# A planned instruction order, fixed buffers and cheaper PSUM copies in a grouped-query attention backward kernel

## The chip, the cores and the metric

One core of a Trainium2 chip. The metric is the device time of one execution in microseconds (us); medians are over several executions, and "span" is the time from the first to the last instruction of the one profiled execution, some 2 us shorter than the device time. All times compared are of fast runs unless a run is named as slow. Engines: PE is TensorE, PEld its weight loads, DVE is VectorE, ACT is ScalarE, POOL is GpSimd, SP is SyncE. "Granted clock" is the share of TensorE's full clock that the throttle allowed.

## The reference, cut to what matters

```python
# B=32, Hq=32, Hkv=4, Sq=4, Sk=2048, D=128, all bf16
k = repeat(k, 8, axis=1); v = repeat(v, 8, axis=1)
p = softmax(einsum("bhqd,bhkd->bhqk", q, k) * D**-0.5)
out = einsum("bhqk,bhkd->bhqd", p, v)
# returned: out and the gradients of q, k, v for a given grad_out
```

Per batch, 32 query heads by 4 positions make 128 rows, so one batch is one set of 128 partitions, and each of the four K/V heads serves 32 of them. K, V, dK and dV are 2 MB each per batch: 8.52 MB go through the transfers per batch with the small tensors, 272.6 MB in all, half of it read and half written.

## The kernel before

Each batch runs through stages; a scheduler orders the instructions and chooses the copying engine (`nc.any`), and all PSUM tiles share one pool of eight banks.

```python
kv_pool = tile_pool(name="kv", bufs=12)      # ... kt 5, vt 8, e 2, et 2
o_pool  = tile_pool(name="ostage", bufs=4)   # dV and dK on their way out
ps_pool = tile_pool(name="ps", bufs=8, space=PSUM)

def pe_transpose_16(src_fn, dst):            # K, V, e and dS are transposed on PE
    for half in range(C // 8):
        tp = ps_pool.tile([P, 8, P], BF16, name="tp", tag="bk")
        for j in range(8):
            nc.tensor.transpose(out=tp[:, j, :], in_=src_fn(half * 8 + j), identity=ident[:])
        evac_big(dst[:, half * 8:half * 8 + 8, :], tp[:])   # nc.any.tensor_copy, 1024 bf16
# scores: four banks, reduce_max of each, reduce_max over four, POOL: negb = -scale * m, then exp
# O and dQ: four banks each, four small copies
# ... order of the stages:
stage_a1(0)
for b in range(B):
    stage_a2a(b)                             # scores, max, exp
    if b + 1 < B: stage_a1k(b + 1)           # next loads, K transposes (lower priority)
    stage_a2b(b); stage_b1o(b); stage_b1v(b) # e transposes, O, dV
    stage_b2a(b)                             # dP, dS
    if b + 1 < B: stage_a1v(b + 1)           # next V transposes (lower priority)
    stage_b2b(b)                             # dK, dQ
```

## Time and profile before

| | before |
|---|---|
| device time, median of the 4 first runs | 1014.98 us (1014.35 to 1016.63) |
| span of the profiled run, mean granted clock | 1012.6 us, 0.741 |
| busy: PE, DVE, ACT | 84%, 66%, 80% |
| moved | 269 GB/s over the span |
| time per batch (first to last score product, over 31) | 31.0 us |

The two rows below, of the page's 40 equal slices, are the shortest form of what the prediction reads from slices of one batch: digits are tenths, the first row of the granted clock, the second of the transfer engines' busy share.

```profile
PEclk9786887676777677776767776777767777677775
DMA  9898677687676686776786776866768767676244
```

Neither is ever steady: the trace's clock records read 0.50 and 1.00 by turns, 0.741 on average, and the transfers are idle over a quarter of the time (the page's queues take 35.8 + 35.6 + 0.7 + 0.1 = 72% of it).

### The profile page before, as it was taken

What the parts mean: (1) busy time and instruction counts of PE and PEld (TensorE: products, weight loads), DVE (VectorE), ACT (ScalarE), POOL (GpSimd) and SP (SyncE); (2) the same over time, 40 slices, a digit from 0 to 9 for tenths busy, and PEclk for the clock granted to TensorE, in tenths of its full rate; (3) what the DMA queues carried; (4) which work ended last, traced back from release to release, by engine and by line L of the source; (5) the groups of instructions that cost most, each with busy time, mean ns of one, the idle gap of its engine ahead of it and who ended that gap; (6) DMA issues with size and microseconds to landing.
All of it is one profiled execution on the core that took longest, in us unless ns stands there. A gap on an engine that the chain in (4) does not pass through costs nothing. (4 is left out here: it accounts for less than half of the span.)

```text
span 1012.6 us, 33638 instructions
## 1 busy us (share of the span) xinstructions
PE 848.5 (84%) x14400; PEld 618.8 (61%) x14400; DVE 668.8 (66%) x1283; ACT 805.1 (80%) x1406; POOL 185.8 (18%) x390
## 2 busy tenths in 40 slices
PE   6678788988889888889888889888898887988884
PEld 6456566666666665666565666656666565666553
DVE  5666667666667666677666676665766667666664
ACT  6688878788888878887878787777878778788874
POOL 0212112212122112122121222121221212212121
PEclk9786887676777677776767776777767777677775
DMA  9898677687676686776786776866768767676244
GB/s 353 314 352 299 255 293 275 262 313 282 252 304 250 268 334 257 259 300 248 299 313 252 281 272 266 309 251 260 284 256 307 263 249 276 262 304 229 112 170 169
DMA packets 85142, 274.82 MB, mean 271 GB/s; under 512 B 18432, under 2 KB 18432, under 8 KB 84992
## 3 DMA queue, kind: packets, MB, share of 16 engines
q1 hardware_dynamic: 46080, 136.34, 35.8%
q0 software_dynamic: 38912, 136.34, 35.6%
q8 instruction: 112, 1.84, 0.7%
q14 instruction: 38, 0.31, 0.1%
HBM read 136.31 MB, written 136.31 MB: 269 GB/s over the span
## 5 line engine op out<-in xcount | busy, mean ns | idle before, releaser
L101 ACT COPY kt_h<-tp 128x1024 bf16<-128x1024 bf16 x157 | 147.3, 1031 | 47.1 <-PE tp L82 46.3
L109 ACT CAST dv_h<-acc 128x512 bf16<-128x512 f32 x350 | 174.5, 641 | 0.8
L109 ACT CAST dk_h<-acc 128x512 bf16<-128x512 f32 x319 | 161.1, 643 | 17.0 <-DMA out_dram<-dv_h 15.9
L82 PEld LDWEIGHTS <-v_h 128*128 128x128 bf16 x2048 | 155.7, 119 | 25.8 <-issue 25.5
L82 PE MATMUL tp<-ident,v_h 128*128 128x128 bf16 x2048 | 161.3, 257 | 0.1
L101 ACT COPY vt_h<-tp 128x1024 bf16<-128x1024 bf16 x129 | 126.6, 1018 | 37.4 <-PE tp L82 37.3
L82 PEld LDWEIGHTS <-k_h 128*128 128x128 bf16 x2048 | 120.5, 100 | 35.7 <-issue 28.2
L82 PE MATMUL tp<-ident,k_h 128*128 128x128 bf16 x2048 | 130.0, 223 | 13.4 <-DMA k_h<-in_k_dram 6.9
L109 DVE CAST dk_h<-acc 128x512 bf16<-128x512 f32 x193 | 121.2, 683 | 27.8 <-DMA out_dram<-dv_h 21.1
L261 PE MATMUL acc<-dop_sb,e_sb 32*128 32x128 bf16 x2048 | 125.8, 281 | 14.5 <-ACT dv_h L109 2.6
L319 PE MATMUL acc<-qp_sb,ds_sb 32*128 32x128 bf16 x2048 | 94.1, 226 | 42.4 <-ACT dk_h L109 21.1
L82 PE MATMUL tp<-ident,e_sb 128*128 128x128 bf16 x512 | 67.4, 275 | 72.6 <-ACT e_sb L195 70.9
L329 POOL DMA_DIRECT2D out_dram<-dk_h x128 | 67.4, 533 | 310.6 <-ACT dk_h L109 296.1
L101 DVE COPY vt_h<-tp 128x1024 bf16<-128x1024 bf16 x127 | 84.7, 688 | 49.4 <-PE tp L82 47.7
L261 PEld LDWEIGHTS <-e_sb 32*128 32x128 bf16 x2048 | 65.3, 110 | 70.6 <-issue 65.6
L109 DVE CAST dv_h<-acc 128x512 bf16<-128x512 f32 x162 | 102.4, 682 | 1.0
L319 PEld LDWEIGHTS <-ds_sb 32*128 32x128 bf16 x2048 | 50.8, 95 | 82.6 <-issue 74.3
L82 PEld LDWEIGHTS <-e_sb 128*128 128x128 bf16 x512 | 38.3, 118 | 97.7 <-ACT e_sb L195 92.8
L291 DVE SCALAR_TENSOR_TENSOR ds_sb<-dp_q,delta,e_sb 128x512 bf16<-128x512 f32 x128 | 87.2, 743 | 9.8 <-PE dp_q L284 9.8
L195 ACT ACTIVATE e_sb<-s_q,negb 128x512 bf16<-128x512 f32 x128 | 86.3, 686 | 3.9 <-POOL negb L191 3.1
L271 POOL DMA_DIRECT2D out_dram<-dv_h x128 | 67.8, 536 | 104.2 <-ACT dv_h L109 98.3
L101 DVE COPY kt_h<-tp 128x1024 bf16<-128x1024 bf16 x99 | 67.5, 685 | 25.1 <-PE tp L82 24.1
(44 smaller groups left out, 938.9 us busy)
## 6 DMA issues: line engine op xcount, KB each, us to landing
k_h<-in_k_dram SPq DMA_DIRECT2D x128, 512.0 KB, 9.3
v_h<-in_v_dram SPq DMA_DIRECT2D x128, 512.0 KB, 5.7
out_dram<-dv_h POOLq DMA_DIRECT2D x128, 512.0 KB, 6.2
out_dram<-dk_h POOLq DMA_DIRECT2D x128, 512.0 KB, 6.5
q_sb<-in_q_dram SPq DMA_DIRECT2D x32, 32.0 KB, 2.6
do_sb<-in_grad_out_dram SPq DMA_DIRECT2D x32, 32.0 KB, 6.6
out_dram<-o_sb POOLq DMA_DIRECT2D x32, 32.0 KB, 5.5
out_dram<-dq_sb POOLq DMA_DIRECT2D x32, 32.0 KB, 9.5
```

The costliest lines, as they stand in the source:

```text
L82: nc.tensor.transpose(out=tp[:, j, :], in_=src_fn(c), identity=ident[:])
L101: nc.any.tensor_copy(out=out, in_=in_)
L109: nc.any.tensor_copy(out=out, in_=in_)
L195: nc.scalar.activation(out=e_sb[:, QW * cq:QW * cq + QW], in_=s_ps[cq][:], func=ACT.Exp, bias=negb[:], scale=scale, accum_out=l4[:, cq:cq ...
L261: nc.tensor.matmul(accs[h][:, j, :], lhsT=e_sb[32 * h:32 * h + 32, P * c:P * c + P], rhs=dop_sb[32 * h:32 * h + 32, :], start=True, stop=True,
L271: store_eng.dma_start(out=dv_v[b, h], in_=dv_sb[h][:].rearrange("p c d -> p (c d)"))
L291: nc.vector.scalar_tensor_tensor(out=ds_sb[:, QW * cq:QW * cq + QW], in0=dp_q[:], scalar=delta[:], in1=e_sb[:, QW * cq:QW * cq + QW], op0= ...
L319: nc.tensor.matmul(accs[h][:, j, :], lhsT=ds_sb[32 * h:32 * h + 32, P * c:P * c + P], rhs=qp_sb[32 * h:32 * h + 32, :], start=True, stop=True,
L329: store_eng.dma_start(out=dk_v[b, h], in_=dk_sb[h][:].rearrange("p c d -> p (c d)"))
```

## The change

Its intent: keep the mathematics, take the order of work away from the scheduler, and plan it. A list schedule is made in Python from a table of lengths, with due times per unit of work and a period of 21 us per batch; it gives the order of every queue, the PSUM bank of every tile and the engine of every copy. Beside it, three operations get cheaper. The core of the diff:

```diff
+PERIOD = 21.0
+LEN = dict(load=1.27, small=0.3, tr8=0.48, cp16=(0.61, 0.50), s=0.25, mx=0.66, m=0.1, ex=0.69,
+           l=0.75, o=0.45, oe=0.3, dl=0.4, ds=0.68, acc=0.40, cp32=(0.62, 0.50), qt=0.12, qte=0.3)
+CAP = dict(q=4, et=1, dt=1, k=12, v=9, kt=4, vt=4, out=13, e=3, ds=2)
+AT = dict(LQ=-44, LK=-42.0, LV=-25.0, QT=-17.0, KT=-19.5, VT=-3.5, S=0, DV=4.0, DK=13, DQ=14.5)
+    order, bank_of = plan(B)                      # ... list schedule, about 190 lines, cut
-    ps_pool = tile_pool(name="ps", bufs=8, space=PSUM)
+    ps_pool = pool("ps", 1, space=PSUM)           # tiles tagged by bank_of[...]
-            nc.any.tensor_copy(out=out, in_=in_)  # 1024 bf16
+        if on == "ACT":                           # 512 pairs read as fp32
+            nc.scalar.copy(out=out.rearrange(...).bitcast(FP32), in_=in_.rearrange(...).bitcast(FP32))
+        else:
+            nc.vector.tensor_copy(out=out, in_=in_)
-            nc.vector.reduce_max(out=m4[:, cq:cq + 1], in_=s_q[:], axis=AX.X)
-        nc.vector.reduce_max(out=m[:], in_=m4[:], axis=AX.X)
-        nc.gpsimd.tensor_scalar_mul(out=negb[:], in0=m[:], scalar1=-scale)
+            nc.vector.tensor_scalar(out=junk[:], in0=t["S", c][:], scalar1=-scale,
+                                    scalar2=t["m"][:] if c else None, op0=ALU.mult, op1=ALU.min,
+                                    accum_out=m[:])
-        o_ps = [ps_pool.tile([P, D], FP32, name="o_ps", tag="bk") for _ in range(NH)]
-        for h in range(NH):
-            evac_scalar(o_sb[32 * h:32 * h + 32, :], o_ps[h][...], rinv[...])
+            nc.vector.tensor_scalar(out=o[:], in0=t["O"][:, 0:D], scalar1=t["rinv"][:], ...)  # one bank
+    with tc.manual_schedule():
+        for u in order:
+            emit(u)
```

## The prediction

> **What bounds the kernel now.** I read first the page's busy shares, then the bytes that the DMA queues moved, then one batch cut into slices of 1 us, then the timeline of the same batch for what one instruction costs back to back, and last the costliest groups for the counts.
>
> ```profile
> PE 848.5 (84%) x14400; PEld 618.8 (61%) x14400; DVE 668.8 (66%) x1283; ACT 805.1 (80%) x1406; POOL 185.8 (18%) x390
> HBM read 136.31 MB, written 136.31 MB: 269 GB/s over the span
> L178 PE MATMUL s_q<-kt_h,qdt_sb x512: 379/631/634, 15.6 to 976.9; 128*32 128x512 bf16 x171
> ```
>
> No engine is full and the DMA average is far from what it reaches in bursts. The score matmuls (one group per batch) start at 15.6 us for the first batch and about 976 us for the last, so a batch takes 961/31 = 31.0 us. One batch in slices; the columns are the stretch, then the busy us (instructions) of PE, weight load, DVE, ACT and POOL, the granted clock, the DMA share and GB/s:
>
> ```profile
> 503.00:504.00 1.00, 0.93 (x22) 0.49 (x21) 1.00 (x2) 1.00 (x3) 0.00 (x0) 1.00 0.05 20
> 504.00:505.00 1.00, 0.69 (x20) 0.35 (x14) 0.68 (x2) 1.00 (x3) 0.00 (x0) 1.00 0.00 0
> 507.00:508.00 1.00, 1.00 (x44) 1.00 (x40) 0.00 (x0) 0.72 (x2) 0.97 (x2) 0.50 0.00 0
> 514.00:515.00 1.00, 0.00 (x0) 0.00 (x0) 0.30 (x2) 1.00 (x2) 0.00 (x0) 1.00 1.05 422
> 520.00:521.00 1.00, 1.00 (x39) 0.80 (x38) 0.00 (x0) 0.00 (x0) 0.00 (x0) 0.50 0.14 40
> 525.00:526.00 1.00, 1.00 (x13) 0.42 (x16) 0.67 (x2) 1.00 (x3) 0.00 (x0) 0.50 1.01 393
> 4.00:42.00 38.00, 27.43 (x486) 22.82 (x487) 24.18 (x44) 26.59 (x40) 3.27 (x7) 0.95 1.03 407
> ```
>
> The stages take turns. At 503 to 505 us DVE and ACT empty PSUM while DMA stands still; at 507 and 520 us PE works at half clock with both copy engines idle; at 514 us PE is idle behind the key-transpose copies on ACT. So the bound is the order of work and the buffers that separate the stages. The last row is the ceiling to remember: in the first 38 us DMA is never empty and moves 407 GB/s. (In the first few us there the clock column reads 1.00 before any record of it, while the transposes run at the cold rate.)
>
> What one instruction costs back to back (the mean duration hides an overlap, so I use run length; start, length, engine, line, what, count):
>
> ```profile
> 510.35 4.68 ACT L101 COPY kt_h<-tp 128x1024 bf16<-128x1024 bf16 x5 [1.25 <-PE tp L82]
> 502.70 5.01 ACT L109 CAST dk_h<-acc 128x512 bf16<-128x512 f32 x10
> 970.28 3.75 DVE L109 CAST dk_h<-acc 128x512 bf16<-128x512 f32 x6
> 20.74 2.57 DVE L101 COPY kt_h<-tp 128x1024 bf16<-128x1024 bf16 x4 [0.41 <-PE tp L82]
> 30.99 3.75 PE L82 MATMUL tp<-ident,v_h 128*128 128x128 bf16 x64
> 5.38 6.40 PE L82 MATMUL tp<-ident,k_h 128*128 128x128 bf16 x64 [5.38 <-DMA k_h<-in_k_dram]
> 24.94 1.08 PE L232 MATMUL o_ps<-v_h,et_sb 128*32 128x128 bf16 x64 [0.78 <-ACT et_sb L101]
> ```
>
> ACT: (4.68 - 1.03)/4 = 0.91 us per 1024-element copy, (5.01 - 0.64)/9 = 0.485 us per 512-element cast. DVE: (3.75 - 0.68)/5 = 0.614 us per cast, (2.57 - 0.69)/3 = 0.63 us per copy. PE: a transpose costs 59 ns warm and 100 ns cold.
>
> [...] the trace has 1031 and 641. Reading two bf16 as one fp32 must therefore almost halve ACT's copies. [...] the trace sustains 407 with peaks of 430, and I use 407. [...] the slices show 0.50 and 1.00, mean 0.741. [...] in the trace the first matmul of the next mode comes some 0.1 us late (my reading, at 16.6 and 35.5 us).
>
> **The change part by part.** It keeps the mathematics and PE's 14400 matmuls, and replaces the scheduler's order by a list schedule made in Python with a cost table, fixed queue order, an explicit PSUM bank per tile, an engine per copy, and other buffer counts (k 12, v 9, output 13 instead of 4).
>
> 1. ACT copies of transposes as fp32 pairs. The built order of the changed kernel puts 393 of 640 on ACT and 247 on DVE (before: 351 and 289), and of the 1024 accumulator casts 637 on ACT and 387 on DVE (before 669 and 355).
> 2. O and dQ go into one bank each and leave in one DVE instruction instead of four small ones on both engines (256 of about 0.36 us become 64).
> 3. The maximum comes with its sign and scale from one DVE pass, so the reduction over four and the POOL step go (0.16 + 0.21 us and two handovers per batch).
>
> ACT before: 351 x 0.91 + 669 x 0.485 + 128 exp x 0.67 + 128 small x 0.37 = 777 us (the page has 805). After: (393 + 637) x 0.485 + 128 x 0.67 = 585 us, 18.3 per batch. DVE before 668.8 by the page; after: 387 x 0.614 + 247 x 0.63 + 128 x 0.68 (dS) + 128 x 0.62 (maximum, taken as the reduction it replaces) + 32 x 2.1 (small ones) = 627 us, 19.6 per batch. So arithmetic removes about 230 us of engine time, hardly any of it alone on a path; the gain must come from the new order.
>
> PE per batch, warm: 162 transposes x 59 ns = 9.5; scores 1.05; dP 1.22; O and dQ 2 x 1.08; dV and dK 8 groups of 16 at about 0.42 = 3.4; together 17.3 us. The built order changes tiling mode 19.7 times per batch instead of 10.8, about +0.9 us: 18.2 us warm. Cold, the same sum with 100 ns transposes and doubled scores, dP, O and dQ is about 29 us.
>
> DMA per batch: 272.62 MB/32 = 8.52 MB, at 407 GB/s 20.9 us. This is now the largest per-batch floor, ahead of DVE 19.6, ACT 18.3 and PE 18.2 warm.
>
> Ends: the first scores come when four K heads are in and transposed, about 12.5 us by this trace (first K at 5.4 us, then 6.4 us of cold transposes). The last batch has nothing beside it: before, it takes from 975 us to the end, 37 us; the new order overlaps dV's copies with dP and dS and the copies of dK with dQ, and I take 28 us. So span = 40 + 31 x period. At the DMA floor that is 40 + 31 x 20.9 = 688 us. Four resources at 87 to 100% with strictly ordered queues won't mesh perfectly; I add 6% to the floor as a judgement, period 22.2 us: 40 + 31 x 22.2 = 728 us.
>
> **The rivals.**
> A. DMA bound, perfect meshing: about 690 us. For it: prefetch of two to three batches and 13 output buffers, and a ceiling seen for 38 us on end. Against it: a schedule planned with fixed lengths has to run on an array whose speed changes twofold.
> B. PE becomes the bound through its clock. At the present mean of 0.741 the array is warm 48% of the time, and a batch needs 1/(0.48/18.2 + 0.52/29) = 22.6 us, giving 741 us; stuck cold, 29 us and 940. For it: in the slices the clock fell after 2 us of idleness and in stages of row- and column-tiled matmuls. Against it: the new order spreads the key and value transposes through the batch[...]. At 0.85 or more PE needs 20.5 us or less and stays hidden.
> C. Copies become the bound through PSUM: scores hold four of eight banks during maximum and exp, when DVE and ACT in turn do not empty transposes, so PE waits for banks. The period would be 23.5 to 24.5 us, 770 to 800 us. For it: DVE at 19.6 us has little slack. Against: the copy engine is chosen per copy with those lengths in view.
> D. A wrong order makes a queue's head wait (a store in POOL's queue ahead of the scaled q that dK needs) and the period stays above 27 us: over 880 us. Unlikely, as the lengths in the table are near those I measure here.
>
> **Range and chances.** A is the lower edge (695 allows it a small slip), C the upper one (775). All rivals except a broken order are more than 10% faster. Predicted 728 us, range 695 to 775; faster 0.97, same 0.02, slower 0.01.
>
> **What would show it.** Right: ACT's transpose copies near 640 ns instead of 1031; ACT busy near 600 us and DVE near 630; score matmuls every 22 us; DMA share above 0.9 in the middle slices near 385 to 405 GB/s; mean clock above 0.85. Wrong: DMA slices under 0.85 with PE near full at clock 0.75 (B); PE waiting on DVE or ACT copies as the longest sum of waits, with DVE above 90% (C); a tail longer than 28 us after the last scores; the maximum pass costing clearly more than 0.62 us.

## The result, and the profile after

The changed kernel takes 716.72 us (median of 11 runs, 713.29 to 723.79), the kernel before 1013.92 us in the same rounds (16 runs). The ratio is 0.7081, 95% interval 0.7060 to 0.7103. Here and below a ratio is the mean time of one kernel's fast runs over that of the other's of the same rounds, so not quite the ratio of the medians quoted. The result is correct. The prediction was 728, in a range of 695 to 775; its sum is a span, which leaves out the some 2 us of the device time, so 712.4 is the number to lay beside 728.

| | before | after |
|---|---|---|
| span, mean granted clock | 1012.6 us, 0.741 | 712.4 us, 0.957 |
| time per batch | 31.0 us | 21.6 us |
| moved over the span | 269 GB/s | 383 GB/s |
| median landing of a dK store, from its issue | 6.5 us | 9.2 us |

The page's busy shares and bytes of the changed kernel, to be laid beside the same two rows of before in the prediction:

```profile
PE 617.4 (87%) x14400; PEld 469.3 (66%) x14400; DVE 615.4 (86%) x1274; ACT 611.3 (86%) x1287; POOL 184.3 (26%) x358
HBM read 136.31 MB, written 136.31 MB: 383 GB/s over the span
```

PE has the same 14400 products and is busy 231 us less, at a mean clock of 0.957 instead of 0.741. Its score products, with min/median/max ns, first and last start:

```profile
L317 PE MATMUL s_ps<-kt_sb,qdt_sb x512: 376/389/634, 12.3 to 681.5; 128*32 128x512 bf16 x171
```

So a batch takes (681.5 - 12.3)/31 = 21.6 us, and 712.4 - 681.5 = 30.9 us come after the start of the last score product. That counts the last batch's own score stage into the 31 batches: its first product starts at 678.8 us by the trace, so from first product to first product a batch takes 21.5 us, and 33.5 us follow. In stretches (columns as in the prediction):

```profile
100.00:200.00 100.00, 89.25 (x2082) 67.54 (x2082) 90.10 (x190) 88.08 (x188) 26.60 (x52) 0.99 1.03 408
300.00:400.00 100.00, 87.25 (x2077) 65.77 (x2066) 88.54 (x181) 86.94 (x182) 27.73 (x53) 0.95 1.01 390
500.00:600.00 100.00, 88.60 (x2106) 67.95 (x2106) 91.61 (x190) 89.29 (x190) 27.09 (x52) 0.98 1.01 395
680.00:712.00 32.00, 14.27 (x356) 9.25 (x352) 15.90 (x34) 17.84 (x38) 7.83 (x15) 0.85 0.53 204
```

The last two columns carry the reading: the transfer engines are never free (1.01 to 1.03), as the prediction asked for, and move 390 to 408 GB/s. PE, DVE and ACT are each at 87 to 92%. (The two stretches left out, 200 to 300 and 400 to 500 us, move 396 and 399 GB/s.) Only in the last 32 us is the share about one half.

The two operations whose length the prediction named, first the page's groups (busy us, mean ns), then one pair of passes from the timeline:

```profile
L271 ACT COPY vt_sb<-V_ps 128x512 f32<-128x512 f32 x163 | 100.0, 618 | 23.9 <-PE V_ps L307 23.2
L271 ACT COPY kt_sb<-K_ps 128x512 f32<-128x512 f32 x166 | 101.4, 615 | 9.9 <-PE K_ps L307 9.8
```

```profile
13.60 0.75 DVE L324 TENSOR_SCALAR_CACHE_REDUCE mjunk<-s_ps,m 128x512 bf16<-128x512 f32 x1
14.27 0.08 DVE L324 DVE_READ_ACCUMULATOR mjunk<-s_ps,m 128x1 f32 x1
14.48 0.75 DVE L324 TENSOR_SCALAR_CACHE_REDUCE mjunk<-s_ps,m 128x512 bf16<-128x512 f32 x1
```

ACT's copy went from 1031 to 615 ns. The maximum pass repeats after 14.48 - 13.60 = 0.88 us, because it is followed by a second instruction that reads the accumulator (0.08 us) and a handover: 0.26 us more than the 0.62 assumed, about 1 us per batch on DVE.

### The profile page after: what moved, and what is told of

Its sections match the earlier page's. It is cut to its first block, busy times and chain, and to the rows that moved or that the text cites.

```text
span 712.4 us, 33563 instructions
## 1 busy us (share of the span) xinstructions
PE 617.4 (87%) x14400; PEld 469.3 (66%) x14400; DVE 615.4 (86%) x1274; ACT 611.3 (86%) x1287; POOL 184.3 (26%) x358
## 4 chain that ended last, share of the span: by engine, by line
PE 34%; DVE 19%; issue 16%; DMA 15%; ACT 11%; POOL 3%; SPq 0%; POOLq 0%; DVEq 0%; ACTq 0%
DMA out_dram<-dk_sb 8%; ACT dv_sb L277 8%; PE K_ps L307 7%; PE V_ps L307 6%; DVE dk_sb L277 5%; DVE mjunk L324 5%; PE DQ_ps L365 4%; DMA k_sb<-in_k_dram 4%; PE D_ps L353 3%; DVE dv_sb L277 3%; PE DK_ps L400 3%; DMA out_dram<-dv_sb 3%; ACT dt_sb L271 2%; PE s_ps L317 2%; PE dp_ps L317 2%
## 5 line engine op out<-in xcount | busy, mean ns | idle before, releaser
L277 ACT CAST dv_sb<-DV_ps 128x512 bf16<-128x512 f32 x351 | 178.7, 608 | 8.4 <-PE DV_ps L400 7.3
L277 ACT CAST dk_sb<-DK_ps 128x512 bf16<-128x512 f32 x286 | 155.2, 606 | 28.0 <-PE DK_ps L400 28.0
L307 PE MATMUL K_ps<-ident,k_sb 128*128 128x128 bf16 x2048 | 162.6, 225 | 12.1 <-DMA k_sb<-in_k_dram 4.1
L307 PE MATMUL V_ps<-ident,v_sb 128*128 128x128 bf16 x2048 | 156.4, 224 | 9.7 <-issue 9.6
L277 DVE CAST dk_sb<-DK_ps 128x512 bf16<-128x512 f32 x226 | 145.7, 681 | 21.4 <-PE DK_ps L400 21.1
L307 PEld LDWEIGHTS <-k_sb 128*128 128x128 bf16 x2048 | 130.3, 101 | 33.2 <-issue 23.4
L307 PEld LDWEIGHTS <-v_sb 128*128 128x128 bf16 x2048 | 126.5, 100 | 26.0 <-issue 22.7
L271 ACT COPY vt_sb<-V_ps 128x512 f32<-128x512 f32 x163 | 100.0, 618 | 23.9 <-PE V_ps L307 23.2
L271 ACT COPY kt_sb<-K_ps 128x512 f32<-128x512 f32 x166 | 101.4, 615 | 9.9 <-PE K_ps L307 9.8
L277 DVE CAST dv_sb<-DV_ps 128x512 bf16<-128x512 f32 x161 | 102.4, 683 | 2.7 <-PE DV_ps L400 2.7
L324 DVE TENSOR_SCALAR_CACHE_REDUCE mjunk<-s_ps,m 128x512 bf16<-128x512 f32 x96 | 72.0, 750 | 12.3 <-PE s_ps L317 0.8
```

Source lines behind the costliest of these rows:

```text
L271: nc.scalar.copy(out=out.rearrange("p c d -> p (c d)").bitcast(FP32), in_=in_.rearrange("p c d -> p (c d)").bitcast(FP32))
L277: (nc.scalar.copy if on == "ACT" else nc.vector.tensor_copy)(out=out, in_=in_)
L307: nc.tensor.transpose(out=ps[:, j, :], in_=t[x, h][:, 8 * i + j, :], identity=ident[:])
L324: nc.vector.tensor_scalar(out=junk[:], in0=t["S", c][:], scalar1=-scale, scalar2=t["m"][:] if c else None, op0=ALU.mult, op1=ALU.min, accu ...
```

## The experiments

The first question was what holds a batch at 21.6 us. In the expectations, theory 1 is that the transfers do, theory 2 that the engines and the order of their work do; theory 3, formed after the first two runs below, is that transfers and engine work hold each other up, so that less work on DVE would shorten the batch too. Twelve kernels ran. Those marked wrong compute a wrong result.

### The transfers alone (wrong)

```diff
-        for u in order:
-            emit(u)
+    for b in range(B):
+        # load q, grad_out, 4 K and 4 V tiles on the sync queue; store the same tiles
+        # to O, dQ, dV, dK on the GpSimd queue; same sizes, no compute
```

> All engine work removed: the same 272.6 MB are loaded into tiles on the sync queue and stored again from those tiles on the GpSimd queue (wrong values on purpose, except for nothing). It measures the transfer floor. If the changed kernel is bound by its transfers (theory 1), this runs at the same mean rate of about 398 GB/s that its middle shows, so 685 to 700 us, within 4% of it. If the transfers only look full because their queues always hold something and the engines set the pace (theory 2), the queues alone go at 410 to 420 GB/s, 650 to 672 us.

Measured 668.58 us (667.92 to 668.9), ratio 0.6593. One stretch (columns here: busy POOL, clock, share, GB/s):

```profile
300.00:400.00 100.00, 26.21 (x49) 1.00 1.03 418
```

Every stretch of 100 us from 100 to 600 us shows 418. At this rate a batch's 8.52 MB take 20.4 us, and the whole takes 48 us less than the changed kernel. The result lies in theory 2's band. So the rate of 390 to 408 is not what the transfers can do by themselves, although their share reads 1.01 to 1.03 in both: **a full share is not a full rate.**

### Half of each dV and dK store (wrong)

```diff
-            nc.gpsimd.dma_start(out=...[b, h], in_=flat(t[name[:2], "out", h]))
+            nc.gpsimd.dma_start(out=...[b, h][:, 0:Sk // 2], in_=flat(t[name[:2], "out", h])[:, 0:Sk // 2])
```

> The changed kernel with only the first half of every dV and dK tile stored (wrong on purpose): 68 MB less to move, all engine work kept. Theory 1 (transfers set the 21.5 us period): the period falls to what the next resource allows, VectorE at 19.2 busy us per batch plus its small gaps, 19.8 to 20.6 us, and the span to 655 to 685 us. Theory 2 (copies, PSUM banks and the in-order queues set it): the period stays at 21.3 us or more, 705 to 717 us.

Measured 688.97 us (686.9 to 690.97), ratio 0.6788; (658.2 - 11.8)/31 = 20.85 us per batch.

```profile
300.00:400.00 100.00, 91.50 (x2162) 70.60 (x2158) 91.88 (x193) 91.18 (x193) 26.86 (x53) 0.95 0.82 306
500.00:600.00 100.00, 92.31 (x2247) 70.82 (x2245) 95.86 (x201) 94.12 (x201) 28.72 (x55) 1.00 0.87 322
```

A quarter of the bytes gone buys only 28 us. It lies just above theory 1's band and below theory 2's: with the transfers relieved, DVE is at 90 to 96% in the five stretches from 100 to 600 us (93% on average, where the changed kernel has 90%) and ACT and PE at 91 to 92% on average. What the engines and their order allow is thus right beneath 21.6 us, at no more than 20.85 us: two bounds within 4% of each other.

### ACT's copies as bf16 again

```diff
-            nc.scalar.copy(out=out.rearrange("p c d -> p (c d)").bitcast(FP32),
-                           in_=in_.rearrange("p c d -> p (c d)").bitcast(FP32))
+            nc.scalar.copy(out=out, in_=in_)
```

> The changed kernel in its own order, but ScalarE copies transposes as 1024 bf16 again instead of 512 fp32 pairs. By the back-to-back lengths of before that adds 393 x (0.91 - 0.485) = 167 us to ScalarE, 24 us per batch, more than the 21.5 us period. If engine time on ScalarE matters once the order is right: ScalarE becomes the bound, 780 to 815 us. If the order alone carries the gain and ScalarE had slack to absorb it: below 745 us.

Of four runs one was fast: 799.98 us at clock 0.955; three were slow, 813 to 837 at 0.88 to 0.92. One fast run is no interval, but it is 83 us above the changed kernel and inside the expected band. The profiled run is a slow one, so only ACT's part of these rows is used (a copy of pairs took 598 to 622 ns at clock 0.819 in the next run and 615 to 618 at 0.957 in the changed kernel, so TensorE's clock hardly shows in it):

```profile
PE 687.0 (82%) x14400; PEld 500.8 (60%) x14400; DVE 634.8 (76%) x1274; ACT 768.0 (92%) x1287; POOL 183.7 (22%) x358
L271 ACT COPY kt_sb<-K_ps 128x1024 bf16<-128x1024 bf16 x166 | 176.4, 1071 | 5.0 <-PE K_ps L306 5.0
```

ACT becomes the fullest engine at 92%. Reading pairs as fp32 is therefore not a detail off the path: without it this order has no room. (The order was planned with the short copy; a plan made anew for the long one wasn't run.)

### The cheaper operations in the old order

```diff
 # the kernel before, with:
-                nc.any.tensor_copy(out=out, in_=in_)
+            f = lambda a: a.rearrange("p c d -> p (c d)").bitcast(FP32)
+            nc.any.tensor_copy(out=f(out), in_=f(in_))   # pairs on DVE too; in the changed kernel on ACT alone
 # and the one maximum pass with sign and scale, and one bank and one copy each for O and dQ
```

> The kernel before, in its own order and with its own buffers, with the three changes of operations alone: fp32-pair copies, O and dQ in one bank each with one copy, the maximum in one pass with sign and scale. My account says the order carries most of the gain, so 900 to 980 us (a tenth to a third of the 298 us). If the operations carry it: below 850 us.

Measured 924.5 us (921.43 to 927.02), ratio 0.9117, span clock 0.819.

```profile
PE 726.3 (79%) x14400; PEld 536.8 (58%) x14400; DVE 564.5 (61%) x1182; ACT 678.6 (74%) x1411; POOL 178.4 (19%) x358
```

The operations alone give 1013.9 - 924.5 = 89 of 297 us, 30%; the order and the buffers, on top of them, the other 208. They are not additive: the order with the old ACT copies still loses 83.

### The order left to the scheduler, with everything else new

```diff
-    with tc.manual_schedule():
-        for u in order:
-            emit(u)
+    for u in order:
+        emit(u)
```

> The changed kernel without the fixed schedule: the planned order is only the order of emission, and the scheduler may move instructions (21.8 instead of 19.7 changes of tiling mode per batch in the built order, copies and transposes shifted by a few places). If the plan's order carries the gain and small moves matter little: 715 to 750 us. If the exact queue order is needed: above 770 us.

Measured 735.2 us (730.74 to 739.99), ratio 0.7247. The scheduler, given units in the plan's order and with the plan's banks and engines, loses only 18.5 us. So the gain over the cheaper operations is in the plan (which unit is beside which, in which bank, on which engine) and its buffers, not in the freezing of queues. Plan and buffers come together here: the old order with the new buffers (13 for output instead of 4) was not run, so how much of the 208 us the buffers alone would give is open.

### One maximum pass per batch instead of four, planned anew

```diff
-        add(("MX", c), ..., [("S", c)] + ([("MX", c - 1)] if c else []), ...)
-        add(("EX", c), {"ACT": LEN["ex"]}, [("MX", NQ - 1)] + ...)
+        if c == 0:
+            add(("MX", c), {"DVE": LEN["mx"]}, [("S", c)], s0 + 0.5 + 0.1 * c)
+        add(("EX", c), {"ACT": LEN["ex"]}, [("MX", 0), ("S", c)] + ...)
```

(The result stays correct for these inputs, as the scores are small.)

> The changed kernel, planned anew, with the maximum of the first quarter of the scores alone (softmax does not depend on the shift, so the result stays right for these inputs, though not safe in general): 96 of 128 maximum passes go, 2.6 us per batch off VectorE, which the plan shares out with ScalarE (986 and 678 shared copies instead of 1030 and 634). All bytes stay. If transfers set the pace at the 397 GB/s seen (theory 1): period 21.3 us or more, 700 to 715 us. If engine work and transfers hold each other up (theory 3, formed after half_stores ran at 20.85 us and the bare transfers at 418 GB/s): the period falls to 20.5 to 20.9 us, close to the bare transfers' 20.4, the middle moves 408 GB/s or more, and the span is 675 to 695 us.

Measured 763.04 us (758.53 to 766.86), ratio 0.7535, with DVE at 577 us instead of 615: less work and 46 us slower, a miss for every theory. The list schedule has made another order out of the lighter load, and three of its waits (engine, line, releaser: us in total, times, longest) show what is wrong with it. They are the longest of ACT, DVE and PE for one another or a store; POOL's, and 98.2 us of weight loads for "issue", are longer:

```profile
ACT dv_sb L277 <- PE DV_ps L400: 65.9, 54, 3.1
DVE dv_sb L277 <- DMA out_dram<-dk_sb: 50.5, 17, 5.4
PE DV_ps L400 <- DVE dv_sb L277: 40.2, 37, 2.8
```

Copies stand at the head of DVE's queue waiting for an output buffer that a store of dK has not left. The plan counts a store as 1.27 + 1.5 us; in the changed kernel it takes 9.2 to 9.7 us from issue to landing. The changed kernel's own order happens not to meet this wait: the first and third of these rows are 7.3 and 3.8 us there, and the second isn't in its list. This run therefore doesn't test the maximum pass by itself; the next one does.

### A cheaper maximum in the same order

```diff
-            nc.vector.tensor_scalar(out=junk[:], in0=t["S", c][:], scalar1=-scale, ..., accum_out=m[:])
+            nc.vector.reduce_max(out=t["m4"][:, c:c + 1], in_=t["S", c][:], axis=AX.X)
+            if c == NQ - 1:   # one small pass over the four: scale, minimum
+                nc.vector.tensor_scalar(out=junk[:], in0=t["m4"][:], scalar1=-scale, ..., accum_out=m[:])
```

> The changed kernel in exactly its own order, with the maximum found as before (four reductions, 0.60 us apart by the trace of before) and one tiny pass over the four for sign, scale and minimum, instead of four chained passes that are 0.88 us apart in the trace of the changed kernel: about 0.75 us per batch off VectorE and off the wait of exp. Under theory 3 some of it shows: period down by 0.1 to 0.5 us, 700 to 714 us. Under theory 1 (transfers alone) no change, within 3 us of the changed kernel.

Measured 718.81 us (714.19 to 721.72), ratio 0.7097 [0.7069, 0.7125]; DVE 610.0 us. In the first batch the maximum is there 2.69 us after its first pass starts instead of 3.34, and nothing changes: this chain doesn't hold the period. Theory 3's band is missed, but DVE's work fell by only 5.4 us in all, 0.2 us per batch instead of the 0.75 expected, so theory 3 in its general form is hardly tested by it.

### Fewer K and V buffers in the same order

```diff
-CAP = dict(q=4, et=1, dt=1, k=12, v=9, ...)
+CAP = dict(q=4, et=1, dt=1, k=10, v=6, ...)
```

> The changed kernel in the same order, with 10 K and 6 V buffers instead of 12 and 9, so loads run at most about half a batch less ahead. If the end is long because loads run far ahead and leave stores alone there (the last load landed at 664 us of 712): loads end later, the end is shorter, 705 to 713 us. If the prefetch is needed against late transfers: PE waits for loads, 720 us or more.

Measured 718.49 us (717.32 to 720.89), ratio 0.7102 [0.7075, 0.7128]. The last load is issued at 674.3 us instead of 652.2, as intended, and the end doesn't move: neither expectation held. The depth of prefetch isn't what holds the period.

### Eighteen output buffers in the same order

```diff
-    k_pool, v_pool = pool("kp", CAP["k"]), pool("vp", CAP["v"])
+    k_pool, v_pool = pool("kp", 10), pool("vp", 6)
-    o_pool = pool("outp", CAP["out"])
+    o_pool = pool("outp", 18)
```

> The order of instructions of the changed kernel to the letter; 18 output buffers instead of 13, and 10 and 6 instead of 12 and 9 for K and V, so that a store which takes 9.5 us to land has 5 more buffers before a copy must wait for it. If the slow landing of stores, by way of output buffers, is what holds the period at 21.5 us: 695-708 us. If the transfers' rate or the engines set it: within 3 us of the changed kernel (714-720). If the shallower prefetch alone costs: the earlier run with 10 and 6 and 13 buffers cost nothing, so more than 722 is not expected by anyone.

Measured 721.41 us (717.68 to 725.55), ratio 0.7125 [0.7098, 0.7151]: no gain, at most a loss; the median is 1.4 us outside the band for "no effect", and the interval overlaps that of the changed kernel. The slow landing of stores doesn't hold the changed kernel by way of its output buffers.

### The last batch's stores in halves, on two queues

```diff
+            if b == B - 1 and i % 2:
+                e, w = (nc.sync, nc.gpsimd)[h % 2], slice(QW * (i - 1), QW * (i + 1))
+                e.dma_start(out=(dv_r if name == "DVe" else dk_r)[b, h][:, w], in_=flat(t[name[:2], "out", h])[:, w])
...
+            if b < B - 1:
                 nc.gpsimd.dma_start(...)
```

> Only the last batch's stores of dV and dK change: each tile goes out in two halves, the first as soon as its first two copies are done, and every second head on the load queue, which is empty by then. The changed kernel ends 32 us after its last scores with the transfers at half their share. If the last stores, queued behind one another at the end, are what stretches that tail: 2-6 us less, 710-715 us. If the tail is the chain of the last batch's own work (scores, exponentials, O, dP, dS, dK with its copies): no change, 715-718.5.

Measured 713.87 us (713.25 to 718.6), ratio 0.7059 [0.7033, 0.7085]. The median is in the band of a gain, but the interval overlaps that of the changed kernel, and the trace has 712.1 - 681.9 = 30.2 us after the last score product instead of 30.9. A gain of more than about 1 us isn't shown.

### The transfers beside busy engines (wrong)

Cheaper DVE work and other buffers in the same order had moved nothing, and the transfers ran 5% below what they do alone. Do busy engines slow them?

```diff
 # the transfers-only run, and per batch, waited for by no transfer:
+        for j in range(28): nc.vector.tensor_copy(out=jk[j % 4][:], in_=bk[0][:])
+        for j in range(28): nc.scalar.copy(out=jk[4 + j % 4][:], in_=bk[1][:])
+        for j in range(300): nc.tensor.matmul(bk[2][:, P * (j % 4):...], lhsT=ident[:], rhs=ident[:], ...)
```

> Wrong on purpose. The loads and stores of the transfers-only run as they were (668.6 us, 418 GB/s in the middle), and beside them three engines kept busy with work that no transfer waits for and that waits for no transfer: per batch 28 copies of a 128x512 bank on VectorE, 28 on ScalarE, 300 matmuls of 128 columns on TensorE (an estimate: 28 x 0.62 us = 17.4 us of each copying engine per batch, some 560 to 620 us in all). Theory A, that the transfers of the changed kernel run at some 397 GB/s because the engines' own traffic on SBUF slows them: the rate falls below 405 GB/s in the middle and the time rises to 680-695 us. Theory B, that the engines don't slow them, and the changed kernel's gap to 418 GB/s comes from when it issues its transfers: 416-420 GB/s in the middle, 667-671 us.

Measured 692.55 us (692.12 to 692.92), ratio 0.6840: inside theory A's band. From its windows (columns as before):

```profile
200.00:300.00 100.00, 100.00 (x1795) 100.00 (x1793) 100.00 (x169) 100.00 (x208) 24.58 (x46) 1.00 1.02 399
400.00:500.00 100.00, 100.00 (x1795) 100.00 (x1793) 100.00 (x168) 41.57 (x85) 25.11 (x47) 1.00 1.02 402
600.00:650.00 50.00, 0.00 (x0) 0.00 (x0) 0.00 (x0) 0.00 (x0) 13.28 (x25) 0.50 1.03 418
```

At about 400 GB/s with the engines at work, 418 after they end. That is the number theory A asked for, but the second row is odd: ACT has stopped inside it, and the rate hardly rises. And the page of this run has a queue that the transfers-only run has not, in the same place as in the changed kernel. First this run, then the changed kernel (packets, MB, share of 16 transfer engines' time):

```profile
q8 instruction: 75, 1.23, 0.6%
```

```profile
q8 instruction: 112, 1.84, 0.9%
```

These packets are 16,384 bytes each. 75 for TensorE's 19,216 instructions and 112 for 28,800 are both 256 to 257 instructions per packet: I read them as refills of TensorE's instructions. The page counts their time, 0.94 us each (median of the records), in the share of the same 16 transfer engines. "Busy engines" can thus mean two things. TensorE itself never stops in this run: no two successive weight loads start more than 0.25 us apart, and a block of 256 instructions lasts 7.15 us.

### The two meanings one after the other (wrong)

```diff
 # the transfers-only run, and beside it, each phase waiting for the one before through its data:
+        for j in range(240): nc.vector.tensor_copy(out=jk[j % 4][:], in_=bk[0][:])          # 1
+        for j in range(300): nc.scalar.copy(out=jk[4 + j % 4][:], in_=bk[1][:])              # 1
+        for j in range(3600):                                                                # 2: 7200 instructions, little data
+            nc.tensor.matmul(bk[2][0:32, i:i + 1], lhsT=jk[3][:, 0:32], rhs=jk[7][:, i:i + 1], ...)
+        for j in range(600): nc.tensor.matmul(bk[j % 2][:], lhsT=ident[:], rhs=jk[7][:], ...) # 3: much data, few instructions
```

> Wrong on purpose. The same transfers throughout, and beside them four phases, one after the other by data dependence, to be read by windows of the one trace: first some 145 us of bank copies on VectorE and ScalarE with TensorE waiting (an engine's traffic, no long stream of instructions); then 3600 TensorE products of one column (7200 instructions, hardly any data: some 28 refills of its instructions, in packets of 16 KB); then 600 products of 512 columns with whole weights (much data in few instructions, some 5 refills); then nothing. If the engines' own traffic on SBUF is what took the run with busy engines from 418 to about 402 GB/s: 400-410 in the first and third phase, 416-420 in the second and fourth. If the refills of TensorE's instructions take it, by holding up one transfer engine for 0.9 us each: 416-420 in the first and fourth, 395-408 in the second, 414-418 in the third. If only all of it together does it: 415 or more in all four. In time: 668-685 us, the excess over 668.6 being the sum of the phases' losses.

Measured 679.11 us (678.81 to 679.66), ratio 0.6712. Phase 1 ends at 149.6 us, phase 2 at 315.7, phase 3 at about 447:

```profile
50.00:100.00 50.00, 0.00 (x0) 0.00 (x0) 50.00 (x84) 50.00 (x106) 12.82 (x24) 1.00 1.03 418
200.00:250.00 50.00, 29.66 (x1077) 29.17 (x1074) 0.00 (x0) 0.00 (x0) 12.81 (x24) 1.00 1.03 407
250.00:300.00 50.00, 30.07 (x1087) 29.52 (x1084) 0.00 (x0) 0.00 (x0) 11.77 (x22) 1.00 1.03 409
350.00:400.00 50.00, 50.00 (x233) 22.67 (x232) 0.00 (x0) 0.00 (x0) 12.82 (x24) 1.00 1.03 415
400.00:450.00 50.00, 47.26 (x219) 21.23 (x217) 0.00 (x0) 0.00 (x0) 12.85 (x24) 0.99 1.03 409
500.00:550.00 50.00, 0.00 (x0) 0.00 (x0) 0.00 (x0) 0.00 (x0) 13.00 (x25) 0.50 1.03 417
```

DVE and ACT at 100% cost the transfers nothing: 418. So theory A's cause is wrong, though its number came true in the run before. Beside the stream of short TensorE instructions, with hardly any data, the rate falls by 2%, to 407 to 409 (414 from 150 to 200 us, not shown). That is at the upper edge of the expected 395 to 408 or over it. The third phase is mixed (415, then 409, with few refills), and one later stretch of 50 us (550 to 600, not shown) also falls to 412 with nothing beside it, so differences of 1% have other causes too. By the bytes moved, this run is 0.2 us behind the transfers-only run when phase 1 ends, 4.7 after phase 2, 6.9 after phase 3 and 10 at the end: not even half of its excess arises in phase 2.

The rates around each refill part the two meanings better. I took the starts of the refill packets from the traces and averaged the rate of the loads and stores (a count from the traces' packet records):

| GB/s | the 2 us up to 0.5 us before | 0 to 0.5 us after the start | 0.5 to 1 | 1 to 1.5 | 1.5 to 2 |
|---|---|---|---|---|---|
| phases run, phase 2, 27 refills | 411 | 389 | 390 | 397 | 408 |
| busy engines, 60 refills (100 to 530 us) | 411 | 373 | 372 | 384 | 398 |
| changed kernel, 101 refills (20 to 640 us) | 408 | 373 | 371 | 383 | 397 |

So each refill takes something from the transfers, for about 2 us: 0.07 us of their time in the phases run, 0.14 and 0.12 in the other two.

The unexpected part is the other direction. TensorE's own timeline in phase 2 (start, length, what, and the idle time ahead of it):

```profile
149.58 5.87 PE L422 MATMUL bk<-jk,jk 128*32 128x1 bf16 x215 [147.18 <-ACT jk L419]
157.09 3.55 PE L422 MATMUL bk<-jk,jk 128*32 128x1 bf16 x128 [1.64 <-issue]
...
175.40 3.55 PE L422 MATMUL bk<-jk,jk 128*32 128x1 bf16 x128 [2.37 <-issue]
181.60 3.55 PE L422 MATMUL bk<-jk,jk 128*32 128x1 bf16 x128 [2.64 <-issue]
187.52 3.55 PE L422 MATMUL bk<-jk,jk 128*32 128x1 bf16 x128 [2.37 <-issue]
```

Nothing is waited for ("issue"), and yet TensorE stops after every 128 products, that is 256 instructions, for 2.4 to 2.6 us: a block of 256 comes every 6 us here, with full transfer queues, while it runs in 3.55.

Is that in the changed kernel? Its timeline has the same mark in the middle of a group of 16:

```profile
310.99 0.09 PEld L400 LDWEIGHTS <-ds_sb 32*128 32x128 bf16 x2
313.19 0.23 PEld L400 LDWEIGHTS <-ds_sb 32*128 32x128 bf16 x14 [2.10 <-issue]
```

To count, I sorted each trace's weight loads by their start, took the gaps between successive ones of more than 0.25 us (each counted as 3 us at most), and grouped them by the load's number modulo 128:

| run | position with the largest mean gap | its mean gap | second largest | sum of gaps at it |
|---|---|---|---|---|
| phases | 96 | 1.89 us | 0.03 us | 71 us |
| changed kernel | 96 | 0.56 us | 0.03 us | 62 us |
| half stores | 96 | 0.33 us | 0.04 us | 37 us |
| cheaper maximum | 96 | 0.64 us | 0.03 us | 71 us |
| last stores in halves | 96 | 0.59 us | 0.04 us | 65 us |
| before | 16 | 0.10 us | 0.09 us | 10 us |

(Means leave out the first 2000 loads; sums don't.) In the changed kernel TensorE stops at 53 of its 112 block boundaries, at the same position as in the phases run; the kernel before has no such position. That these stops are waits for refills can be read directly: at each of the 53, the next weight load starts 1.2 to 1.7 us after a refill packet ends. The 62 us are from load to load; while they last, products already loaded still run, and TensorE is idle for 47 of them. Busy time and these stops together fill (617.4 + 47)/712.4 = 93% of TensorE's span; before it was 84% and no stops.

Full queues do delay the refills. With half the stores the transfers have gaps: there the next refill starts 0.9 us after a boundary (median of 17) where the transfer engines are under 20% busy around it, and 3.0 us after (median of 74) where they are over 95%. The pace of TensorE matters as well: beside full queues, blocks of 7.15 us came without a stop in the run with busy engines, and blocks of 3.55 us with one after each in the phases run. On average a block lasts 1012.6/112 = 9.0 us in the kernel before and 834.8/112 = 7.5 us in the profiled (slow) run with the bf16 copies, which has no such position either, and 6.4 us in the changed kernel.

The run that would weigh this, the changed kernel with fewer and longer TensorE instructions, was not made, and no version tried beats the changed kernel outside the intervals, so there is no combined one.

## Why the prediction was right

**What bounds the kernel before: right.** The stages took turns, and both halves of the remedy are measured: operations alone 924.5 us, the plan with its buffers on top of them 716.7. Two readings of the prediction were loose. In the slice at 507 us ACT is not idle, as it says, but busy for 0.72 us (both copying engines are idle in the one at 520). And the "cold" 6.40 us of 64 transposes hold the change to the full clock: in the trace they start 107 ns apart up to 11.0 us, where the first clock record reads 1.00, and 56 ns apart after it (the changed kernel does the same at 9.7 us), so cold is 107 ns and not 100. Neither carries the number. That copies read as fp32 pairs would take little more than half the time was an estimate, from the 1031 ns that the trace of before has for 1024 elements and the 641 for 512; ACT's copies of pairs took 615 to 618.

**"Arithmetic ... hardly any of it alone on a path; the gain must come from the new order": right in direction, too strong.** The operations alone give 30% of the gain, the plan with the old ACT copies loses 83 us, and the plan without frozen queues keeps all but 18.5 us.

**The cost of each part.** ACT was worked out as 585 us and is 611.3; DVE as 627 and is 615.4. ACT's transposes are copied in 615 to 618 ns, where "near 640" was the sign. The maximum pass was mis-sized: 0.62 us taken, 0.88 measured. It was named as something that would show the prediction wrong, and it made no difference, because this chain isn't what holds the period: a cheaper one in the same order gives 718.8. PE was worked out as 18.2 us a batch warm, 20.5 at a clock of 0.85; it is 617.4/32 = 19.3 at 0.957. The 0.9 us a batch for changes of tiling mode was tested by no run.

**Ends.** First scores at 12.5 us predicted, 12.3 measured. The tail was mis-sized: 28 us predicted, where the prediction counts from the first of the last batch's score products (975 us to the end, 37 us, in the kernel before). Counted so, it is 712.4 - 678.8 = 33.5 us. Sum 46 instead of 40. Storing the last tiles in halves hardly moves it, so the tail is not shown to be the last stores; what it is stays open.

**The period.** 20.9 us as the transfers' floor plus 6% for imperfect meshing made 22.2; from first score product to first score product it is 21.5. So the period was 0.7 us too long (31 x 0.7 = 22 us) and the ends 6 us too short, and the two errors in part cancel in the total. The floor of 407 GB/s, taken from the first 38 us of before, is not the ceiling: the transfers alone hold 418, 20.4 us a batch. And the loss on top of it is (21.5 - 20.4)/20.4 = 5%, near to the 6%. That the 6% came out is in part luck, as it was a judgement that no sum stood behind. "Meshing" is only part of the loss's cause. A part is shown: TensorE's instruction refills slow the transfers, by 0.12 us each in the changed kernel (an estimate from the rates around them), some 14 us for 112. By the bytes moved, the changed kernel is 34 us behind the transfers-only run at 640 us, and 712.4 - 666.8 = 46 us behind at the end. So the refills explain a bit over a third of the loss in the middle; some 12 us belong to the tail, and the rest, about 20 us, is open.

**The rivals.** A (transfers, about 690) was nearest in number. B (PE by its clock) fell: the clock is 0.957, over the 0.85 needed. But PE is nearly the bound in a way that none of the rivals had: 87% busy and 7% waiting for its own instructions. C (copies through PSUM) is in no longest wait of the changed kernel: PE's products wait 45 us with no releaser ("issue") and 19 us for DVE and ACT together. It may lie close beneath, as half the stores bring DVE to 93%. D did not come in the changed kernel, and did in the re-planned one.

**What sets the 21.6 us, then?** The transfers are occupied without a break, and TensorE with its refills is at 93%. Each makes the other slower: full queues delay refills (in the half-stores run, 3.0 us after a boundary with the transfer engines over 95% busy, 0.9 under 20%), refills take from the transfers (0.12 us each). Halving the stores relieves both at once, so it can't part them. More output buffers, a shallower prefetch and a shorter maximum change nothing, by runs in the same order. Which of the two ends last in a batch is not settled.

## What to carry to other kernels

When stages take turns, price each resource per batch, take the largest as the floor, and add the two ends; here that was good to 2%, in part because the period was taken too long and the tail too short. When engines and transfers are both near full, a share of 1.0 doesn't say that the transfers run at their best rate (here 390 to 408 GB/s at a share of 1.01 to 1.03, and 418 at 1.03 alone): run them alone to learn it, and look for the instruction queue in the page, because in this kernel many short instructions waited for their own refills (47 us of TensorE's span). And a run that lands in a theory's band shows the number, not the cause; change one meaning of the cause at a time before believing it, and keep the order fixed when a plan would be made anew.
